# Chunked attention and a quadratic-relu FFN in one kernel: the first tiles' q and k are loaded four tokens to a partition and turned in 64x64 blocks

## The chip, the cores and the metric

The kernel runs on one core of one Trainium2 chip. The metric is the device time of one launch in microseconds, lower is better. The kernel before takes 829.1 us, the median of three runs (827.03 to 829.47). Engines are named as in the profile: PE is TensorE (matrix products), PEld its weight loads, DVE VectorE, ACT ScalarE, POOL GpSimd, SP the engine that issues most DMAs.

## The reference

Attention works inside chunks of 64 tokens, for 8 batches, 8 heads, 576 tokens and 64 channels. Its output, in token order, is the input of a feed-forward layer of 512 to 2048 to 512 with a quadratic ramp between.

```python
q_c, k_c, v_c = (x.reshape(B, H, nc, 64, D) for x in (q, k, v))
scores = q_c @ k_c.transpose(0, 1, 2, 4, 3) / sqrt(D)
attn = exp(scores - max(scores)); attn = attn / (sum(attn) + 1e-9)
x = (attn @ v_c).reshape(B, H, S, D).transpose(0, 2, 1, 3).reshape(B * S, H * D)
h = x @ w_in
g = where(h >= 1, h, where(h <= -1, 0, (h + 1) ** 2 / 4))
return g @ w_out
```

## The kernel before

**Tiles.** The 4608 tokens are cut into nine tiles of 512: tiles 0 to 5, 7 and 8 are the first 512 tokens of one batch each, tile 6 the last 64 tokens of all eight batches (`BATCH`). The attention of a tile is done in four head groups of two heads, each an array of 128 x 512. The feed-forward layer goes by 16 column blocks `j` of w_in and w_out. All its products are made from numbers split in a high and a low part, with three products in place of one.

**Attention of a group.** q and k arrive with tokens on the partitions and must have channels there. Three ways exist: PE multiplies by an identity matrix (`flip`, L436, four transposes of 128x128 for q and four for k) and ACT copies the result out (L461); or DVE transposes 32x32 blocks (L452) after a load in blocks (L371, L384 and others). `by_row(t, g)` says which: tile 0 and, of tile 1, the groups in `ROWED` go by PE. Then come the scores (L478), the exponent and its normalization (L552 to L570; by POOL at tile 0), the turning back of the weights (L436 with e, copied at L581), the product with v (L496), and the split of the result into xh (L613) and xl (L614).

**Feed-forward.** Tiles 0 to 2 run it directly: `ffn_in` (L665) and `ffn_out` (L700), twelve products of 128x512 for each block. Tiles 3 to 8 run in pairs with fewer products: `ffn_quad` (L880) works on combinations of weights that were mixed during tile 2 and written to DRAM (`mix_weights`, L761; read back L811), and half of its values are held in DRAM (L904) until the second tile of the pair recalls them (L939). The four token quarters of a tile accumulate in four PSUM banks, `ps_o` 0 to 3: 0 and 1 are tiles of their own, 2 and 3 one tile, `ps_o23`. At the end of a tile `store` evicts them, even quarters by ACT (L729), odd ones by DVE (L727), into the ring of four `tmp` buffers, which the held values use too, and SP sends them (L738).

**Weights** arrive in fp32 words by DMA (L296, L303) and are split by ACT and DVE in `prepare` (L320 to L342).

**The order.** A planner collects every piece of work with a cost and what it reads and writes, and lays the instructions out for each engine by estimated times, in the order they were added where it can; `plan.behind` ranks pieces later. While PE has no products in the start-up, it is filled with products of the identity (`warm`, L1105).

## Time and profile before

| | us |
|---|---|
| median of 3 runs | 829.1 |
| profiled execution | 828.9 |
| its span | 827.1 |
| PE busy | 819.0 (99%) |
| DVE busy | 563.2 (68%) |
| ACT busy | 422.5 (51%) |
| POOL busy | 153.8 (19%) |

The span is what the engines' records cover; the rest of the execution's time lies around it. Shares are means over stages: PE has work or filler nearly throughout, DVE and ACT are near full in the first 130 us, while the weights are prepared, and half idle at the end. A row of the timeline gives start, duration, engine, line, operation, written<-read, and in brackets how long the engine was idle before, and what ended that.

### The profile page before, as it was taken

What the parts mean: (1) busy time and instruction counts of PE and PEld (TensorE: products, weight loads), DVE (VectorE), ACT (ScalarE), POOL (GpSimd) and SP (SyncE); (2) the same over time, 40 slices, a digit from 0 to 9 for tenths busy, and PEclk for the clock granted to TensorE, in tenths of its full rate; (3) what the DMA queues carried; (4) which work ended last, traced back from release to release, by engine and by line L of the source; (5) the groups of instructions that cost most, each with busy time, mean ns of one, the idle gap of its engine ahead of it and who ended that gap; (6) DMA issues with size and microseconds to landing.
All of it is one profiled execution on the core that took longest, in us unless ns stands there. A gap on an engine that the chain in (4) does not pass through costs nothing.

```text
span 827.1 us, 15446 instructions
## 1 busy us (share of the span) xinstructions
PE 819.0 (99%) x5786; PEld 676.7 (82%) x5786; DVE 563.2 (68%) x965; ACT 422.5 (51%) x723; POOL 153.8 (19%) x278
## 2 busy tenths in 40 slices
PE   9999999999999999999999999999989999999998
PEld 8778878888888888888888888888878888888886
DVE  4889998857778888786787748775756254454422
ACT  5899965444445465455464344544544254454422
POOL 1222112222221111112122111121122121121220
PEclk9999999999999999999999999999999999999999
DMA  9998886554697546979597738875663264552432
GB/s 203 285 314 294 247 195 156 137 124 101 170 242 150 124 102 175 260 179 262 167 226 231 175 108 214 216 190 188 164 223 95 63 207 157 168 169 86 157 98 77
DMA packets 278683, 146.80 MB, mean 177 GB/s; under 512 B 243152, under 2 KB 251600, under 8 KB 278608
## 3 DMA queue, kind: packets, MB, share of 16 engines
q1 hardware_dynamic: 251584, 61.25, 33.7%
q0 software_dynamic: 24768, 83.90, 31.0%
q10 hardware_dynamic: 2256, 0.66, 0.5%
q8 instruction: 46, 0.75, 0.4%
q14 instruction: 29, 0.24, 0.1%
HBM read 101.71 MB, written 36.70 MB: 167 GB/s over the span
## 4 chain that ended last, share of the span: by engine, by line
PE 88%; DMA 4%; issue 2%; DVE 2%; SPq 2%; POOL 1%; ACT 0%; ACTq 0%; POOLq 0%; DVEq 0%
PE ps_o L700 43%; PE ps_h L880 26%; PE ps_h L665 13%; PE ps_a L478 2%; PE ps_h L496 2%; PE ps_a L700 1%; DMA words_wo<-in_moe_w_out_dram 1%; DMA v_sb<-in_v_dram 1%; DMA q_sb<-in_q_dram 1%; SPq L409 1%; DMA held<-tmp 1%; SPq L359 1%; DMA k_sb<-in_k_dram 1%; PE ps_a L436 0%; PE ps_o L665 0%
## 5 line engine op out<-in xcount | busy, mean ns | idle before, releaser
L700 PE MATMUL ps_o<-parts_wo,gh 128*128 128x512 f32 x1120 | 347.9, 392 | 2.2 <-DVE tmp L727 2.2
L700 PEld LDWEIGHTS ps_o<-parts_wo,gh 128*128 128x128 f32 x1120 | 208.6, 188 | 46.2 <-DVE tmp L727 2.8
L700 PE MATMUL ps_o<-parts_wo,gl 128*128 128x512 f32 x560 | 218.4, 390 | 0.0
L880 PE MATMUL ps_h<-big_wi,big_wi 128*128 128x512 f32 x720 | 172.3, 389 | 0.0
L880 PEld LDWEIGHTS ps_h<-big_wi,big_wi 128*128 128x128 f32 x720 | 135.2, 188 | 28.0
L665 PE MATMUL ps_h<-xh,parts_wi 128*128 128x512 f32 x376 | 125.4, 394 | 0.1
L686 DVE TENSOR_TENSOR gl<-r,gh 128x512 fp32r<-128x512 f32 x120 | 82.4, 687 | 60.9 <-ACT gh L685 60.1
L700 PEld LDWEIGHTS ps_o<-parts_wo,gl 128*128 128x128 f32 x560 | 105.2, 188 | 22.4 <-DVE gl L686 0.3
L685 ACT CAST gh<-r 128x512 fp32r<-128x512 f32 x120 | 74.2, 619 | 96.0 <-PE ps_o L700 55.8
L811 POOL DMA_DIRECT2D big_wi<-mixed x84 | 44.9, 535 | 264.1 <-PE ps_h L880 251.7
L665 PEld LDWEIGHTS ps_h<-xh,parts_wi 128*128 128x128 f32 x376 | 70.6, 188 | 16.1 <-DVE r L676 0.5
L665 PE MATMUL ps_h<-xl,parts_wi 128*128 128x512 f32 x188 | 73.6, 391 | 0.4 <-DVE xl L614 0.4
L894 ACT ACTIVATE tmp<-big_wi 128x512 f32<-128x512 f32 x48 | 30.3, 632 | 71.4 <-DVE big_wi L889 70.0
L880 PE MATMUL ps_h<-xh,big_wi 128*128 128x512 f32 x192 | 63.5, 390 | 0.0
L672 ACT ACTIVATE r<-ps_h 128x512 f32<-128x512 f32 x47 | 27.9, 597 | 43.6 <-PE ps_h L665 43.4
L889 DVE TENSOR_TENSOR big_wi<-ps_h,big_wi 128x512 f32<-128x512 f32 x48 | 32.9, 685 | 19.0 <-PE ps_h L880 13.8
L898 DVE SCALAR_TENSOR_TENSOR tmp<-big_wi,tmp 128x512 f32<-128x512 f32 x48 | 33.2, 692 | 15.9 <-ACT tmp L897 15.8
L676 DVE SCALAR_TENSOR_TENSOR r<-ps_h,r 128x512 f32<-128x512 f32 x47 | 32.1, 682 | 16.1 <-ACT r L675 15.9
L880 PEld LDWEIGHTS ps_h<-xh,big_wi 128*128 128x128 f32 x192 | 36.1, 188 | 7.7 <-DVE e L889 0.2
L665 PEld LDWEIGHTS ps_h<-xl,parts_wi 128*128 128x128 f32 x188 | 35.3, 188 | 7.7 <-DVE xl L614 0.7
L761 POOL DMA_DIRECT2D mixed<-e x32 | 17.2, 543 | 127.2 <-ACT e L790 127.2
L904 POOL DMA_DIRECT2D held<-tmp x48 | 26.4, 550 | 72.6 <-DVE tmp L898 72.5
(150 smaller groups left out, 1030.9 us busy)
## 6 DMA issues: line engine op xcount, KB each, us to landing
big_wi<-mixed POOLq DMA_DIRECT2D x84, 512.0 KB, 4.0
held<-tmp POOLq DMA_DIRECT2D x48, 256.0 KB, 3.8
words_wi<-in_moe_w_in_dram SPq DMA_DIRECT2D x16, 512.0 KB, 6.6
words_wo<-in_moe_w_out_dram SPq DMA_DIRECT2D x16, 512.0 KB, 7.5
out_dram<-tmp SPq DMA_DIRECT2D x31, 256.0 KB, 3.3
aT_both<-qT_both SPq DMA_DIRECT2D x112, 64.0 KB, 2.8
v_sb<-in_v_dram SPq DMA_DIRECT2D x52, 128.0 KB, 3.7
q_sb<-in_q_dram SPq DMA_DIRECT2D x104, 64.0 KB, 3.5
```

What stands on the lines that cost most here:

```text
L665: nc.tensor.matmul(out=ps, lhsT=weight["wi", j][:, half, kc * P:(kc + 1) * P], rhs=x, start=(kc == 0 and i == 0), stop=(kc == KC - 1 and i ...
L672: plan.add("act", 0.48, lambda: nc.scalar.activation(out=r, in_=ps, func=AF.Relu, bias=0.5, scale=0.5), (pkey,), (rkey,))
L676: plan.add("dve", 0.6, lambda: nc.vector.scalar_tensor_tensor(out=r, in0=ps, scalar=1.0, in1=r, op0=ALU.max, op1=ALU.min), (pkey,), (rkey,))
L685: plan.add("act", 0.52, lambda: nc.scalar.copy(out=gh, in_=r), (rkey,), (ghkey,))
L686: plan.add("dve", 0.6, lambda: nc.vector.tensor_tensor(out=gl, in0=r, in1=gh.bitcast(F32), op=ALU.subtract), (rkey, ghkey), (glkey,), port ...
L700: nc.tensor.matmul(out=acc, lhsT=x[:, cols], rhs=weight["wo", j][:, half, :], start=(j == 0 and i == 0), stop=(j == NF - 1 and i == 2),)
L811: plan.add("pool", 0.65, lambda: nc.gpsimd.dma_start(out=place_of(f"wi{slot}").bitcast(F32), in_=mixed[u]), keys, (f"wi{slot}_0", f"wi{slo ...
L880: nc.tensor.matmul(out=bank, lhsT=w[:, c:c + P], rhs=x()[:, kc, :], start=start and kc == 0 and k == 0, stop=kc == 1 and k == 2, skip_grou ...
L889: plan.add("dve", 0.6, lambda: nc.vector.tensor_tensor(out=out(), in0=bank, in1=x(), op=ALU.add), (key, xkey), (out_key,))
L894: plan.add("act", 0.5, lambda: nc.scalar.activation(out=r, in_=h(), func=AF.Relu, bias=0.5, scale=0.5), (hkey,), (rkey,))
L898: plan.add("dve", 0.6, lambda: nc.vector.scalar_tensor_tensor(out=r, in0=h(), scalar=1.0, in1=r, op0=ALU.max, op1=ALU.min), (hkey,), (rkey,))
L904: plan.add("pool", 0.65, lambda: nc.gpsimd.dma_start(out=held[j], in_=r), (rkey,), (f"held{j}",), lag=2.1, moving=0.8)
```

## The change

1. **Loads by rows.** `load_rows` sends one DMA for q or k of a group; partition p holds tokens 4p to 4p+3 of both heads, in runs of 1 KB. Before there were two DMAs (four at tile 1) with runs of 256 bytes. ACT issues k of groups 0 and 2, before of 0 and 1.
2. **Turning.** `flip_rows` turns q and k of a group together with 32 products of 64x64 blocks with the identity, into a pair of banks. The copies out of it put the tokens in order again: they write with a step of four elements. k of tile 0's groups 0 and 1 is copied by DVE, all other by ACT.
3. **Tile 1's group 1** goes by DVE's transposes instead of PE's.
4. **`ps_o` 0 and 1** become one tile of two banks, as 2 and 3 are.
5. **Start-up order.** The softmax is cut into `attn_exp` and `attn_norm`, and the stages of tile 0 stand in a string (T turn, S scores, A exponent, N normalization, B turn back, V product with v, X split, W split of weights). The turning back of groups 0 and 1 uses a bank of `ps_h`.
6. **`store`**: the last quarter of tiles 3, 5 and 7 is evicted to `e_bufs[0]` instead of the ring.
7. **`mix_weights`**: the three plain copies of a weight part to DRAM come behind the mixed ones and wait for their buffer.
8. One burst of attention stands at block 7 instead of 8, and softmax and turning back in a burst are ranked later by 22.

```diff
     FLIPPED, TURNED = 2, 1
-    ROWED = (0, 1)
...
-    o_pair, a_pair = bank_pair("ps_o23"), bank_pair("ps_a")
-    o_banks = buffers(psum, "ps_o", 2) + [(f"ps_o{2 + b}", o_pair[:, b, :]) for b in range(2)]
...
     def load_rows(dst, src, t, g, queue):
-        dst = dst.rearrange("p (c d) -> p c d", d=D)
-        for j in range(2):
-            queue.dma_start(
-                out=dst[j * C:(j + 1) * C],
-                in_=heads_rows(src, t, 2 * g + j).rearrange("c p d -> p c d"),
-            )
-    def load_halves(dst, src, t, g, queue):
-        dst = dst.rearrange("p (u r d) -> p u r d", r=2, d=D)
-        for j in range(2):
-            rows = heads_rows(src, t, 2 * g + j).rearrange("(r u) p d -> r p u d", r=2)
-            for r in range(2):
...
-            load = load_values if n == "v" else load_rows if t < TURNED else load_halves if by_row(t, g) else load_blocks
-            parts = (8 if t == TURNED else 4) if load == load_blocks else 4 if load == load_halves else 2
-            if BATCH[t] is None or (n, t) == ("v", TURNED):
+            load = load_values if n == "v" else load_rows if by_row(t, g) else load_blocks
+            parts = (8 if t == TURNED else 4) if load == load_blocks else 1 if load == load_rows else 2
+            if BATCH[t] is None or n == "v" and by_half(t, g):
...
-            issuer, queue = ("act", nc.scalar) if (n, t) == ("k", 0) and g < 2 else ("sp", nc.sync)
+            issuer, queue = ("act", nc.scalar) if (n, t) == ("k", 0) and g in (0, 2) else ("sp", nc.sync)
...
+    def flip_rows(pair, q_rows, k_rows):
+        for r in range(NS):
+            for n, x in enumerate((q_rows, k_rows)):
+                for a in range(2):
+                    for h in range(2):
+                        rows, at = slice(a * C, (a + 1) * C), h * HALF + r * D
+                        to = n * HALF + r * C
+                        nc.tensor.matmul(
+                            out=pair[h * D:(h + 1) * D, a, to:to + C],
+                            lhsT=x[rows, at:at + D], rhs=ident[rows, rows], start=True, stop=True,
+                        )
...
+    turned, ended = {}, {}
+    POOLED = (0, 1, 2, 3)
+    COPIED = ((0, 0, 1), (0, 1, 1))
...
+        pair, pkeys = ((o_pairs[0], ("ps_o0", "ps_o1")), (a_pair, ("ps_a0", "ps_a1")))[t]
+        plan.add("pe", 0.75, lambda: flip_rows(pair, *(src for (_, src), _ in sides)),
+                 [skey for (skey, _), _ in sides], pkeys, columns=1024, lag=0.0)
+        for n, (_, (dkey, dst)) in enumerate(sides):
+            by_dve = (t, g, n) in COPIED
+            eng = nc.vector.tensor_copy if by_dve else nc.scalar.copy
+            turned[n] = plan.add(
+                "dve" if by_dve else "act", 0.6 if by_dve else 0.48,
+                lambda n=n, dst=dst, eng=eng: eng(
+                    out=dst.rearrange("p (a u r) -> p a r u", a=2, r=NS),
+                    in_=pair[:, :, n * HALF:(n + 1) * HALF].rearrange("p a (r u) -> p a r u", r=NS),
+                ),
                 pkeys, (dkey,), lag=late(t, 1.5),
             )
             if t == 0:
-                turned[n] = copy
+                ended[0] = turned[n]
...
+    def attn_norm(t, g):
+        skey, sm = room("sm", sm_bufs, t, g)
+        ekey, e = e_room(t, g)
+        e3 = e.rearrange("p (n k) -> p n k", k=C)
...
-        on_pool = t < 1
+        on_pool = t == 0 and g in POOLED
...
-            pkey, ps = o_banks[1] if t == 0 else a_banks[0]
+            pkey, ps = (h_banks if g < 2 else o_banks)[1] if t == 0 else a_banks[0]
...
                 okey, o = (e_bufs[0], r_bufs[0])[by_dve]
+            elif t >= PAIRED and (t - PAIRED) % 2 == 0 and s == NS - 1:
+                okey, o = e_bufs[0]
             else:
...
-        for n, kc, which in ((i, 0, 1), (i, 1, 2), (j, 1, 4)):
-            to_mixed(m, which, [(None, keys[n], lambda n=n, kc=kc: weight["wi", n].bitcast(F32)[:, :, kc * HALF:(kc + 1) * HALF])])
...
+        for n, kc, which in ((i, 0, 1), (i, 1, 2), (j, 1, 4)):
+            to_mixed(m, which, [(None, (*keys[n], bkey), lambda n=n, kc=kc: weight["wi", n].bitcast(F32)[
+                :, :, kc * HALF:(kc + 1) * HALF
+            ])])
...
-        ("q", 0), ("k", 0), ("q", 1), ("k", 1), ("q", 2), ("k", 2), ("wi", 0), ("q", 3), ("k", 3),
-        ("v", 0), ("v", 1), ("wi", 1), ("v", 2), ("v", 3),
+        ("q", 0), ("k", 0), ("q", 1), ("k", 2), ("k", 1), ("q", 2), ("wi", 0), ("v", 1),
+        ("q", 3), ("k", 3), ("v", 0), ("wi", 1), ("v", 2), ("v", 3),
...
+    in_turn = (
+        "T0 S0 A0 T1 S1 N0 A1 N1 T2 S2 B0 V0 T3 S3 A3 A2 X0 B1 V1 N2 X1 B2 N3 B3 "
+        "V2 V3 W0 W2 X2 X3 W1"
+    )
+    for stage, n in in_turn.split():
+        stages[stage](int(n))
...
-    FIRST_SCORES, BURSTS = 4, (4, 8, 11, 15)
+    FIRST_SCORES, BURSTS = 4, (4, 7, 11, 15)
...
+        plan.behind = 22
         for at in then:
             attn_softmax(*at)
         if then:
             attn_turn_back_pair(then)
+        plan.behind = 0
```

SP's queue at the start, where the first loads are issued (L359 loads q and k, L296 weights, L409 v; `first_wi` are parts of weight space that hold groups 2 and 3). Before:

```order
L359 DMA q_sb_70<-in_q_dram 64x8x64 x2
L359 DMA q_sb_71<-in_q_dram 64x8x64 x2
L359 DMA first_wi_109<-in_q_dram 64x8x64 x2
L359 DMA first_wi_111<-in_k_dram 64x8x64 x2
L296 DMA words_wi_190<-in_moe_w_in_dram 128x4x256
L359 DMA first_wi_109<-in_q_dram 64x8x64 x2
L359 DMA first_wi_111<-in_k_dram 64x8x64 x2
L409 DMA v_sb_74<-in_v_dram 128x4x64 x2
L409 DMA v_sb_75<-in_v_dram 128x4x64 x2
```

And now (L360, L297, L401):

```order
L360 DMA q_sb_70<-in_q_dram 128x2x256
L360 DMA q_sb_71<-in_q_dram 128x2x256
L360 DMA k_sb_73<-in_k_dram 128x2x256
L360 DMA first_wi_108<-in_q_dram 128x2x256
L297 DMA words_wi_174<-in_moe_w_in_dram 128x4x256
L401 DMA v_sb_75<-in_v_dram 128x4x64 x2
L360 DMA first_wi_108<-in_q_dram 128x2x256
L360 DMA first_wi_110<-in_k_dram 128x2x256
L401 DMA v_sb_74<-in_v_dram 128x4x64 x2
```

Two DMAs of a tensor have become one; k of group 1 now goes by SP and k of group 2 by ACT, and v of group 1 comes ahead of group 3's q and k.

PE's first instructions after the warm-up, where group 0 of tile 0 is turned and its scores made (L436 and L478 before):

```order
L436 MATMUL ps_o_106<-ident,k_sb_72 128x128 x4
L1105 MATMUL ps_h_107<-ident 128x128
L436 MATMUL ps_o_105<-ident,q_sb_70 128x128 x4
L1105 MATMUL ps_h_107<-ident 128x128 x4
L478 MATMUL ps_a<-kT_78,qT_both 64x64 x16
L436 MATMUL ps_o_106<-ident,k_sb_73 128x128 x4
```

Now (L439 turns, L493 scores):

```order
L439 MATMUL ps_o_103<-ident,q_sb_70 64x64 x4
L439 MATMUL ps_o_103<-ident,k_sb_72 64x64 x4
...
L1130 MATMUL ps_h_106<-ident 128x128 x5
L493 MATMUL ps_a<-kT_78,qT_both 64x64 x16
L439 MATMUL ps_o_103<-ident,q_sb_71 64x64 x4
L439 MATMUL ps_o_103<-ident,k_sb_73 64x64 x4
```

The eight transposes of 128x128 into two tiles are now eight rows of four 64x64 products into one; the scores follow both.

DVE around the end of tile 5, with the engines and DMA queues whose work each instruction waits for (L727 is the eviction; `ps_o_106` and `ps_o_103` hold quarters 1 and 3 of the tile). Before:

```order
L898 SCALAR_TENSOR_TENSOR r_94<-e_80,r_94 128x512 [waits DVE_49,Activation_49]
L686 TENSOR_TENSOR gl_98<-r_94,gh_96 128x512 [waits PE_49,Activation_49]
L898 SCALAR_TENSOR_TENSOR tmp_99<-big_wi_161,tmp_99 128x512 [waits Activation_49]
L686 TENSOR_TENSOR gl_97<-r_93,gh_95 128x512 [waits DMASW5_49,PE_49,Activation_49]
L727 COPY tmp_101<-ps_o_106 128x512 [waits DMASW2_49,PE_49]
L686 TENSOR_TENSOR gl_98<-big_wi_161,gh_96 128x512 [waits DMASW1_49,PE_49,Activation_49]
L727 COPY tmp_99<-ps_o_103 128x512 [waits DMASW3_49,DVE_49,PE_49]
```

Now (L749; `ps_o_103` and `ps_o_104` are the two pairs):

```order
L921 SCALAR_TENSOR_TENSOR r_94<-e_80,r_94 128x512 [waits DVE_49,Activation_49]
L921 SCALAR_TENSOR_TENSOR tmp_99<-big_wi_160,tmp_99 128x512 [waits DVE_49,Activation_49]
L706 TENSOR_TENSOR gl_98<-r_94,gh_96 128x512 [waits PE_49,Activation_49]
L706 TENSOR_TENSOR gl_97<-r_93,gh_95 128x512 [waits DMASW7_49,PE_49,Activation_49]
L749 COPY tmp_101<-ps_o_103 128x512 [waits DMASW2_49,Activation_49]
L749 COPY e_80<-ps_o_104 128x512 [waits Activation_49]
L706 TENSOR_TENSOR gl_98<-big_wi_160,gh_96 128x512 [waits DMASW1_49,Activation_49]
```

Quarter 3 goes to `e_80` and no longer waits for a DMA; both evictions wait for ACT, where quarter 1 waited for PE; and they now stand next to each other, with one of the L686 rows (now L706) behind.

More of the change, by code (lines that the diff above doesn't have):

```diff
@@ L192 @@
     FLIPPED, TURNED = 2, 1
-    ROWED = (0, 1)
+    ROWED = (0,)
     EARLY = 2
@@ L238, in bank_pair @@
         return psum.tile([P, 2, T], F32, name=name)
-    o_pair, a_pair = bank_pair("ps_o23"), bank_pair("ps_a")
-    o_banks = buffers(psum, "ps_o", 2) + [(f"ps_o{2 + b}", o_pair[:, b, :]) for b in range(2)]
+    o_pairs, a_pair = [bank_pair("ps_o01"), bank_pair("ps_o23")], bank_pair("ps_a")
+    o_pair = o_pairs[1]
+    o_banks = [(f"ps_o{b}", o_pairs[b // 2][:, b % 2, :]) for b in range(4)]
     a_banks = [(f"ps_a{b}", a_pair[:, b, :]) for b in range(2)]
@@ L475, in product @@
             rows = slice(half * C, (half + 1) * C)
-            at = i * HALF + n * C if t == TURNED and not by_row(t, g) else (2 * n + i) * C
+            at = (i * HALF + n * C if by_half(t, g)
+                  else (n // 2 * 4 + 2 * i + n % 2) * C if by_row(t, g) else (2 * n + i) * C)
             at = slice(at, at + C)
@@ L492, in product @@
         def product(n, h, half):
-            at = (2 * n + h) * C if t < FLIPPED else h * HALF + n * C
+            at = (2 * n + h) * C if by_half(t, g) else h * HALF + n * C
             of = h * HALF + n * C
@@ L1111 @@
         (warm(h_banks[0][1]), None, plan.written["ps_h0"][0]),
-        (warm(o_banks[0][1]), turned[0], plan.written["ps_o0"][NP]),
+        (warm(o_banks[0][1]), ended[0], plan.written["ps_o0"][NP]),
     )))
```

62 lines of the change are left out of this document (26 added, 36 removed).

## The prediction

> **What bounds the kernel now.** I read the shares of busy time first, then TensorE's own list of waits, then stretches of the span.
>
> ```profile
> PE 819.0 (99%) x5786; PEld 676.7 (82%) x5786; DVE 563.2 (68%) x965; ACT 422.5 (51%) x723; POOL 153.8 (19%) x278
> ...
> PE ps_o L700 <- DVE tmp L727: 2.2, 1, 2.2
> PE ps_h L1105 <- POOL ident masks.py:199: 1.4, 1, 1.4
> PE ps_h L665 <- DVE xl L614: 0.4, 1, 0.4
> PE ps_a L436 <- DMA q_sb<-in_q_dram: 0.2, 1, 0.2
> ...
> 0.00:10.00 10.00, 8.64 (x83) 8.45 (x84) 0.83 (x2) 2.76 (x4) 0.70 (x6) 1.00 1.00 163
> 10.00:20.00 10.00, 9.88 (x192) 9.13 (x192) 8.10 (x18) 7.74 (x15) 2.48 (x3) 1.00 1.01 242
> 20.00:31.00 11.00, 10.64 (x144) 8.12 (x144) 9.56 (x18) 8.60 (x17) 4.08 (x5) 1.00 0.92 277
> 60.00:70.00 10.00, 10.00 (x76) 8.01 (x75) 8.64 (x16) 10.00 (x20) 1.45 (x2) 1.00 1.05 400
> 100.00:110.00 10.00, 10.00 (x104) 8.09 (x104) 10.00 (x19) 8.12 (x15) 1.45 (x2) 1.00 0.88 228
> 480.00:620.00 140.00, 137.82 (x1021) 113.84 (x1020) 94.51 (x155) 68.69 (x115) 26.93 (x50) 1.00 0.67 192
> 780.00:827.10 47.10, 43.28 (x190) 35.19 (x188) 12.10 (x18) 10.87 (x19) 5.91 (x11) 1.00 0.34 106
> ```
>
> TensorE is busy for 819.0 of 827.1 us. Its whole list of waits has four rows and 4.2 us, one of them a single wait of 2.2 us on an eviction by VectorE. The rows of stretches give span, then PE, PEld, DVE, ACT and POOL busy, granted clock, DMA share and GB/s. TensorE lacks 2.18 us between 480 and 620 and 3.82 at the end; the clock is 1.00 throughout. In the first 31 us a full PE means little, since it is filled with warm-up products on the identity (L1105). So time can change in three places only: the start-up until TensorE runs on real work, the few holes behind it, and the tail. Elsewhere only products removed or added count. The matmuls of 128x512 follow each other by 0.23 us (22.08 for 96 in the row below).
>
> **The change part by part.** *The hole at 616.*
>
> ```profile
> 606.75 0.68 DVE L898 SCALAR_TENSOR_TENSOR r<-e,r 128x512 f32<-128x512 f32 x1
> ...
> 612.27 0.55 POOL L904 DMA_DIRECT2D held<-tmp  x1
> ...
> 614.59 1.21 PE L496 MATMUL ps_h<-aT_both,v_sb 64*64 64x64 f32 x64
> ...
> 617.23 0.69 DVE L727 COPY tmp<-ps_o 128x512 f32<-128x512 f32 x1 [2.74 <-DMA held<-tmp]
> ...
> 617.98 0.73 PE L700 MATMUL ps_o<-parts_wo,gh 128*128 128x512 f32 x2 [2.18 <-DVE tmp L727]
> ...
> 612.27 4.84 DMA held<-tmp
> ...
> 617.98 22.08 PE ps_o L700 x96
> ```
>
> The eviction of tile 5's last quarter needs a buffer of the tmp ring, and that buffer's content is still being written to DRAM: issued at 612.27, landed 4.84 later, at 617.11. TensorE has finished the value products of L496 at 615.80 and stands until 617.98. For tiles 3, 5 and 7 the change sends just this quarter to e_bufs[0]. Its last use in this pair is the row at 606.75, and VectorE stands idle for 2.74 us before 617.23, that is from 614.49, so the wait is gone, unless VectorE has something else ahead of it. **−2.2 us.** Cases of tiles 3 and 7 show no DMA wait on TensorE's list, and gain nothing. What is late next is the ordinary order of the evictions, which the next item makes longer.
>
> *Accumulators 0 and 1 in one pair of banks.* Their evictions, one by ScalarE, one by VectorE, no longer overlap each other's products: VectorE's now waits for ScalarE's, and ScalarE's for the products of both. Accumulators 2 and 3 are such a pair already, so the trace has a price.
>
> ```profile
> 779.49 0.59 ACT L729 COPY tmp<-ps_o 128x512 f32<-128x512 f32 x1 [1.45 <-PE ps_o L700]
> 780.11 0.69 DVE L727 COPY tmp<-ps_o 128x512 f32<-128x512 f32 x1 [1.29 <-ACT tmp L729]
> 780.42 0.39 PE L700 MATMUL ps_o<-parts_wo,gl 128*128 128x512 f32 x1
> ...
> 780.86 0.73 PE L700 MATMUL ps_o<-parts_wo,gh 128*128 128x512 f32 x2
> ...
> 610.62 0.59 ACT L729 COPY tmp<-ps_o 128x512 f32<-128x512 f32 x1 [0.28 <-PE ps_o L700]
> ...
> 611.30 0.69 DVE L727 COPY tmp<-ps_o 128x512 f32<-128x512 f32 x1 [0.24 <-PE ps_o L700]
> ...
> 612.46 0.62 PE L700 MATMUL ps_o<-parts_wo,gh 128*128 128x512 f32 x2
> ```
>
> At 780.42 to 780.86 two products stand 0.44 apart instead of 0.23: 0.21 us for one such chain. For accumulators 0 and 1 at 611: the products of accumulator 1 end at about 611.26, ScalarE takes 0.59 and VectorE 0.69 with some 0.04 between each, which reaches 612.66, against 612.46 when the next product on that bank is due now. That is 0.2 us again. It comes up where the next tile's products follow at once, behind tiles 1, 3, 5 and 7: 4 x 0.22 = **+0.9 us**. Below: 0 where the scheduler put other work between. Above: all eight boundaries, 1.8.
>
> *The tail.*
>
> ```profile
> 821.33 0.59 ACT L729 COPY tmp<-ps_o 128x512 f32<-128x512 f32 x1 [3.00 <-PE ps_o L700]
> ...
> 821.94 1.69 SPq L738 DMA_DIRECT2D out_dram<-tmp  x3
> ...
> 823.82 0.33 SPq L738 DMA_DIRECT2D out_dram<-r  x1
> ```
>
> ScalarE's first eviction waits for accumulator 1 too, about 0.68 us (the next quarter's products end that much later), and SP's three sends of 0.56 each begin at 822.6 instead of 821.94. They then run to 824.3, and the last send by SP moves from 823.82 to 824.3: **+0.5 us**; 0 if the ScalarE queue's own last send, which does not move, ends later.
>
> *Tile 1, group 1 by VectorE.*
>
> ```profile
> 53.12 0.63 PE L436 MATMUL ps_a<-ident,q_sb 128*128 128x128 f32 x4 [0.18 <-DMA q_sb<-in_q_dram]
> 53.51 0.71 PE L700 MATMUL ps_o<-parts_wo,gh 128*128 128x512 f32 x2
> ...
> L452 DVE STREAM_TRANSPOSE qT_both<-q_sb x30: 668/699/712, 76.0 to 549.6; 128x512 f32<-128x512 f32 x30
> ```
>
> Two groups cost TensorE four turns now, each 0.39 by the start of what follows (53.51 − 53.12), so 1.56 us, plus the wait of 0.18. One group in the new form is 32 products of 64x64 for q and k together. The row at 614.59 has that many in 1.21 (the trace records each product on float32 operands of this size twice, x64). So −1.74 + 1.21 ≈ **−0.5 us**. VectorE gains two transposes of 0.70. It is full there (10.00 of 10 from 100 to 110), so the cover is thin: nothing if TensorE has other products queued, 1.4 if all of it passes through. I take +0.3, near the lower end, since no TensorE wait on VectorE appears now between 31 and 615.
>
> *Start-up.* Three edits meet here.
>
> ```profile
> 6.95 0.60 PE L436 MATMUL ps_o<-ident,q_sb 128*128 128x128 f32 x4
> ...
> 7.59 0.58 ACT L461 COPY qT_both<-ps_o 128x512 f32<-128x512 f32 x1
> ...
> 8.37 0.70 PE L478 MATMUL ps_a<-kT,qT_both 64*64 64x64 f32 x32
> ...
> 28.03 0.66 ACT L320 ACTIVATE tmp<-words_wo 128x512 f32<-128x512 f32 x1 [1.24 <-DMA words_wo<-in_moe_w_out_dram]
> ...
> 30.64 0.50 PE L665 MATMUL ps_h<-xl,parts_wi 128*128 128x512 f32 x1 [0.36 <-DVE xl L614]
> ...
> L326 ACT ACTIVATE words_wi<-words_wi 128x512 uint32<-128x512 uint32 x16 | 10.9, 679 | 0.0
> ...
> L338 ACT CAST parts_wi<-tmp 128x512 fp32r<-128x512 f32 x16 | 10.0, 624 | 1.7 <-DVE tmp L331 1.7
> ```
>
> (1) Loads. The DMA engines are full in the first 10 us (share 1.00) at 163 GB/s, and full at 400 GB/s between 60 and 70, with other pieces. The first q and k are in 256-byte pieces now and in 1024-byte ones after. They let the turn of q start at 6.95 today; between no gain and the whole ratio of the rates I take 4.8 to 5.3 for both tensors. (2) Turn and copies. Today they are two turns of 0.60, and ScalarE copies the one while TensorE turns the other. The new turn is one row of 1.2, and behind it k's copy (VectorE, 0.69) and q's (ScalarE, 0.59) follow each other, since they read one pair of banks. The first scores come at about 5.0 + 1.2 + 0.7 + 0.6 + 0.2 = 7.7 instead of 8.37. (3) The same lengthening comes three times more, for groups 1 to 3, while DVE is busy 9.56 and ACT 8.60 of 11 us from 20 on; so what the first group gains is paid back in part. Against it, the weights no longer queue behind slow pieces and the early DMA copies of POOL, and ScalarE's wait of 1.24 at 28.03 goes. What counts is when the product at 30.64 runs, since TensorE has no further wait until 53.12: I take **−0.2 us**, from −2.5 (loads and the wait passed through in full) to +4 (below).
>
> *A rule that speaks against it.* The copies that undo the order write with a step of 16 bytes. The nearest row is L326, which steps by 8 bytes on both sides: 0.679 against 0.624 of the contiguous L338, so a step of 8 costs 9%; I price the copies as today, plus 0.05. The Trainium skill ("Advanced Engine Details and Errata", "SBUF Cachelines") says that accesses should hit a 16-byte line at least twice, and that a new line with each access is penalized; at a step of 16 every element has its own line. By this rule the copies would take longer by an amount that the page doesn't state, which is the case of the second rival below; by the row the sum stays as it is. No copy with this step is in the trace of before, so the trace neither agrees nor disagrees.
>
> *POOL's late copies* to DRAM and the burst list: POOL is idle in most of the span (19% busy), and its reads of mixed weights wait for TensorE.
>
> ```profile
> L811 POOL DMA_DIRECT2D big_wi<-mixed x84 | 44.9, 535 | 264.1 <-PE ps_h L880 251.7
> ```
>
> 251.7 of the 264.1 us ahead of these reads are waits on TensorE, so a copy that comes later is covered; without that cover each costs its 0.54 of issue. I take 0.
>
> **Sum**: 828.9 (the profiled execution; span 827.1 and 1.8 around it) − 2.2 + 0.9 + 0.5 − 0.5 + 0.3 − 0.2 = 827.7. The profiled execution lies 0.2 under the median of the runs, 829.1.
>
> **The rivals.** *The loads carry through* (0.30). The start-up is bound by what the DMAs land, as share 1.00 in 0 to 10 and ScalarE's wait at 28.03 say. Then about 2.5 us come off in place of 0.2: 827.7 − 2.3 = 825.4. Against it: ACT and DVE are near full from 20 to 31, so an early landing meets a queue.
>
> *The strided copies are twice as long* (0.12): the side on which the kernel becomes slower. Eight copies of tile 0 at 1.2 instead of 0.59 to 0.69, six on ScalarE and two on VectorE, lie one behind the other in the chain of turn, scores and exponent, with ScalarE idle only 2.4 us between 20 and 31. 8 x 0.55 = 4.4, less 0.4 of idle that I let absorb it: 827.7 + 4.0 = 831.7. It decides from about 1.6 times the length on, where the loss passes the hole that was closed. For it: nothing in this trace writes by 16 bytes. Against: step 8 costs 9% only.
>
> *VectorE becomes the bound of tile 1* (0.11): two more transposes where it is full, 1.4 instead of 0.3, and the attention of tile 1 late by as much: 828.8.
>
> *The hole stays* (0.07): the eviction waits for something else, for example ScalarE's of its pair or the send that emptied e_bufs[0] last: 827.7 + 2.2 = 829.9. The row at 606.75 speaks against it.
>
> **How the numbers follow.** The forecast keeps 0.40, with 826.4 to 828.9 for its own range. 0.3% of 829.1, about what a measurement of this kernel can tell from no change, is 2.5 us: faster is below 826.6, slower above 831.6. Faster: 0.27 of the carried-through loads and a fifth of the forecast, 0.35. Slower: 0.09 of the strided copies and 0.03 of the others, 0.12. The same: 0.53. The range of 8 in 10 reaches from the loads' case with no price for the pair of banks (825.4 − 0.9 = 824.5) to just under the strided copies at full length, 831.3.
>
> **What would show it.** The hole: no row of TensorE waiting on an eviction near 615, and the eviction writes e. The pair: gaps of 0.2 behind ScalarE's evictions, four of them. The start: the copies by their mean duration (0.6 or 1.2), the first scores at 7.7, no wait of ScalarE on words_wo, and the last product that waits on xl at 30.4 instead of 30.64. Tile 1: a TensorE row waiting on a VectorE transpose or its scores near 95 would be the third rival. The forecast is wrong if the product that ends the start-up moves by more than 1 us either way, or if a new wait above 1 us stands anywhere on TensorE's list.

## The result

The changed kernel takes **836.4 us** (median of six runs, 834.23 to 838.1), the kernel before 828.6 in the same session (six runs, 827.03 to 832.57). The ratio is **1.0091**, 95% interval 1.0071 to 1.0111: slower by 7.8 us, where 827.7 and a range up to 831.3 were forecast. The profiled execution took 837.1, its span is 835.3.

The shares of busy time in the page of the changed kernel, and the five longest of TensorE's eight waits:

```profile
PE 823.3 (99%) x6066; PEld 680.1 (81%) x6066; DVE 564.4 (68%) x969; ACT 422.4 (51%) x719; POOL 153.7 (18%) x278
```

```profile
PE ps_o L493 <- issue: 2.0, 1, 2.0
PE ps_h L1130 <- POOL ident masks.py:199: 1.4, 1, 1.4
PE ps_a L493 <- ACT qT_both L472: 1.0, 1, 1.0
PE ps_h L903 <- DVE e L912: 0.9, 1, 0.9
PE ps_o L493 <- ACT first_wi L472: 0.8, 1, 0.8
```

TensorE has 280 instructions more (5786 before). The 2.2 us on the eviction at the end of tile 5 are gone. New are waits for the copies of the turned q and k (L472), one on VectorE's e, and one of 2.0 us with nothing named as its cause ("issue"). All but that on e lie in the first 25 us (the three that are not shown are of 0.3 to 0.4, in the start-up too). TensorE's timeline there (start, duration, engine, line, operation, written<-read):

```profile
1.37 5.07 PE L1130 MATMUL ps_h<-ident 128*128 128x128 f32 x22 [1.37 <-POOL ident masks.py:199]
6.36 0.41 PE L439 MATMUL ps_o<-ident,q_sb 64*64 64x64 f32 x8
...
9.89 0.69 PE L493 MATMUL ps_a<-kT,qT_both 64*64 64x64 f32 x32 [0.99 <-ACT qT_both L472]
...
21.97 0.68 PE L493 MATMUL ps_o<-first_wi,first_wo 64*64 64x64 f32 x26 [0.77 <-ACT first_wi L472]
24.69 0.49 PE L493 MATMUL ps_o<-first_wi,first_wo 64*64 64x64 f32 x6 [2.04 <-issue]
...
27.83 2.75 PE L1130 MATMUL ps_o<-ident 128*128 128x128 f32 x12
...
40.03 0.39 PE L685 MATMUL ps_h<-xl,parts_wi 128*128 128x512 f32 x1
```

The first scores begin at 9.89 (8.37 before), those of group 3 at 21.97 (18.18). These 32 rows are the 16 products of the program: the trace has two instructions for each of them, as for the products of the turns and the fillers, and the counts below are of such instructions. Behind the 26th TensorE stops for 2.04 us. The 12 filler instructions after it take 2.75; in a run below the same 12 take 1.50. The last row is the 20th product of 128x512, the one that stood at 30.64 before: 9.4 us late. The copies, in ScalarE's and VectorE's rows of this kernel:

```profile
7.66 1.09 DVE L472 COPY kT<-ps_o 128x512 f32<-128x512 f32 x1 [7.66 <-PE ps_o L439]
...
8.78 1.05 ACT L472 COPY qT_both<-ps_o 128x512 f32<-128x512 f32 x1 [5.71 <-DVE kT L472]
```

They take 1.05 to 1.13. Before, ScalarE's took 0.57 to 0.59; VectorE had none, and its copies of 128x512 out of PSUM take 0.69. The stretches (span; PE, PEld, DVE, ACT, POOL busy; clock, DMA share, GB/s):

```profile
15.00:20.00 5.00, 4.24 (x168) 3.86 (x162) 3.67 (x8) 3.54 (x6) 0.93 (x1) 1.00 0.90 287
20.00:25.00 5.00, 2.19 (x60) 1.78 (x52) 2.15 (x4) 4.09 (x6) 1.04 (x1) 0.86 1.02 352
25.00:30.00 5.00, 5.00 (x25) 4.61 (x21) 3.84 (x9) 1.67 (x3) 1.57 (x2) 0.50 1.09 373
30.00:35.00 5.00, 5.00 (x66) 4.09 (x68) 2.65 (x6) 3.40 (x6) 0.51 (x1) 0.96 1.07 397
```

From 20 to 25 TensorE is busy for 2.19 of 5 us, and from 25 to 30 the granted clock is 0.50. That is why fillers and products take nearly twice as long there. The DMA engines are full from 20 on.

How late the big products (128x512) of the changed kernel are against the same products before, counted in the two traces:

| product | before, us | after, us | late by |
|---|---|---|---|
| 1st | 21.91 | 26.40 | 4.5 |
| 20th | 30.64 | 40.03 | 9.4 |
| 50th | 37.60 | 46.83 | 9.2 |
| 200th | 75.67 | 86.75 | 11.1 |
| 500th | 154.37 | 161.47 | 7.1 |
| 1600th | 421.79 | 428.93 | 7.1 |
| 2000th | 516.96 | 524.59 | 7.6 |
| 2400th | 612.23 | 621.38 | 9.2 |
| 2500th | 638.53 | 645.79 | 7.3 |
| end of span | 827.12 | 835.32 | 8.2 |

Behind the 50th the change gains 1.0 us in all: 2.1 until the 500th, 1.9 at the hole of tile 5, less 0.5, 1.5 and 0.9. The whole loss is made in the first 31 us of the kernel before. A single trace is good to about 1 us there: in three runs below that have the start-up of the kernel before (the eviction buffer, items 6 and 8, and the same order), the 20th product stands at 29.4 to 29.8 and not at 30.64.

### The profile page after: what moved, and what is told of

Same layout as the page of the kernel before. It is cut to its first block, busy times and chain, and to the rows that moved or that the text cites. A ratio compares the mean times of both kernels' runs of the same rounds, so it can differ in the third digit from the quotient of the medians.

```text
span 835.3 us, 15975 instructions
## 1 busy us (share of the span) xinstructions
PE 823.3 (99%) x6066; PEld 680.1 (81%) x6066; DVE 564.4 (68%) x969; ACT 422.4 (51%) x719; POOL 153.7 (18%) x278
## 4 chain that ended last, share of the span: by engine, by line
PE 96%; ACT 1%; DMA 1%; DVE 1%; SPq 1%; issue 1%; POOL 0%; POOLq 0%; DVEq 0%
PE ps_o L720 46%; PE ps_h L903 26%; PE ps_h L685 16%; PE ps_a L493 2%; PE ps_h L511 2%; PE ps_a L720 1%; DMA aT_both<-qT_both 1%; PE ps_h L1130 1%; PE ps_o L1130 1%; SPq L614 1%; PE ps_o L439 1%; ACT first_wo L472 0%; PE ps_o L685 0%; PE ps_a L511 0%; PE ps_o L493 0%
## 5 line engine op out<-in xcount | busy, mean ns | idle before, releaser
L706 DVE TENSOR_TENSOR gl<-r,gh 128x512 fp32r<-128x512 f32 x120 | 82.2, 685 | 68.7 <-ACT gh L705 68.0
```

The lines of the kernel that those rows point to most:

```text
L706: plan.add("dve", 0.6, lambda: nc.vector.tensor_tensor(out=gl, in0=r, in1=gh.bitcast(F32), op=ALU.subtract), (rkey, ghkey), (glkey,), port ...
```

## The experiments

Ratios are against the kernel before, run on the same chip (medians 828.4 to 829.6), with their 95% intervals.

### Copies and loads

The theory after the first look: the copies' stores with a step of 16 bytes are the loss.

**Copies without a step.** Source and destination contiguous.

```diff
-                    out=dst.rearrange("p (a u r) -> p a r u", a=2, r=NS),
-                    in_=pair[:, :, n * HALF:(n + 1) * HALF].rearrange("p a (r u) -> p a r u", r=NS),
+                    out=dst.rearrange("p (a x) -> p a x", a=2),
+                    in_=pair[:, :, n * HALF:(n + 1) * HALF],
```

> The changed kernel with its order of instructions kept; only the copies behind the new turns write straight on instead of with a step of 16 bytes. They leave out putting the tokens of tile 0 and of tile 1's first head group back in order, so those rows of the output are other rows. Copy theory (the copies of 1.09 us instead of 0.59 set the start-up, and the hole and half clock of TensorE around 23 to 30 us are their consequence): copies at 0.6, third scores some 3 us earlier, the twentieth big product near 32 instead of 40, clock 1.00, 828 to 829 us. Fetch theory (TensorE runs out of fetched instructions at 22.65, whatever the copies take, and the clock halves for it): copies at 0.6, but a gap of about 2 us inside a group of score products stays and the mean clock stays under 0.998: 832 us. If the copies stay at 1.09, the step isn't their cause: 836.

**The step on the side of the read.** The order is undone while reading PSUM; the store is contiguous.

```diff
-                    out=dst.rearrange("p (a u r) -> p a r u", a=2, r=NS),
-                    in_=pair[:, :, n * HALF:(n + 1) * HALF].rearrange("p a (r u) -> p a r u", r=NS),
+                    out=dst.rearrange("p (a u r) -> p a u r", a=2, r=NS),
+                    in_=pair[:, :, n * HALF:(n + 1) * HALF].rearrange("p a (r u) -> p a u r", r=NS),
```

> The changed kernel with its order kept; the copies put the tokens in order by reading PSUM with a step of 64 elements and writing straight on. Result as the reference's. If only the write's step of 16 bytes costs: copies 0.6 and the time of the run with plain copies. If any step costs, in PSUM too: copies near 1.1 and 836 us.

**Fewer products.** 16 products of 128 rows and 64 columns instead of 32 of 64x64, with copies as in the change.

```diff
-        for r in range(NS):
-            for n, x in enumerate((q_rows, k_rows)):
-                for a in range(2):
...
-                            lhsT=x[rows, at:at + D], rhs=ident[rows, rows], start=True, stop=True,
+        for n, x in enumerate((q_rows, k_rows)):
+            for r in range(NS):
...
+                        out=pair[h * D:(h + 1) * D, n, r * P:(r + 1) * P], lhsT=x[:, at:at + D], rhs=ident, start=True, stop=True,
```

> The changed kernel with 16 products of 128x64 with 128 columns per group for the turn instead of 32 of 64x64 with 64 columns; copies as in the change (step of 16 bytes), other work the same. Copy theory: the turn is a little shorter, 835 to 836, hole and half clock stay. Fetch theory: 80 instructions fewer before 22 us, the hole of 2.0 us inside the score products is gone or comes later, clock nearer 1.00, 831 to 832.

Measured: 836.2 (1.0077, 1.0052 to 1.0103), 835.0 (1.0065, 1.0047 to 1.0082) and 837.3 (1.009, 1.0067 to 1.0114). The copies of the second kernel by group (count, shortest/median/longest in ns), and then its timeline at the place of the hole:

```profile
L472 ACT COPY first_wo<-ps_o x3: 586/586/587, 9.8 to 17.0; 128x512 f32<-128x512 f32 x3
L472 DVE COPY kT<-ps_o x1: 691/691/691, 7.4 to 7.4; 128x512 f32<-128x512 f32 x1
```

```profile
18.22 0.68 PE L493 MATMUL ps_o<-first_wi,first_wo 64*64 64x64 f32 x26
21.77 0.49 PE L493 MATMUL ps_o<-first_wi,first_wo 64*64 64x64 f32 x6 [2.88 <-issue]
```

Reading with the step costs nothing (0.59 and 0.69); the step of the stores cost 0.5 and 0.4 each. Group 3's scores begin at 18.22, as before the change. But the hole behind the 26th instruction is now 2.88 us. In the first run it is at the same instruction, 3.70 long and ends at 23.66. So most of the gain of the copies goes into the hole. Against the kernel before of its own session the second run is slower by 5.5 us, the changed kernel by 7.8: 2.3 are gained, with intervals of 1.5 and 1.7 to either side. 828 to 829 were expected, and the theory of the copies alone falls. (The profiled execution of the second run is the fastest of its eight, so its trace shows the hole rather too short.)

The third run has no hole in that place, but its turn takes longer:

```profile
16.70 1.97 PE L437 MATMUL ps_o<-ident,first_wi 128*64 128x128 f32 x32
```

1.97 instead of 1.11 for q and k of a group. The 64x64 products in four quarters of the array overlap (in the changed kernel the first four start at 6.36, 6.37, 6.37 and 6.38), these do not. So this edit does not stand for "fewer instructions" alone.

**Both undone.** Fewer products and the step on the read.

> The changed kernel with both suspects taken away at once: 16 turns of 128x64 per group instead of 32 of 64x64, and copies that write straight on (they read PSUM with a step). Two-cause theory (slow copies and the late block of instructions hide each other, since the chain that is behind arrives at the block's boundary later): no hole marked issue above 0.5 us on TensorE, clock 1.00, copies 0.6, the twentieth big product at 31 to 33 us instead of 35.9 with the copies alone and 38.9 with the turns alone; time 829 to 831 us, 5 to 7 less than the changed kernel. Rival (the order of the stages itself is slower): the start-up stays 5 us or more behind, 834 or more.

Measured: 836.9 (1.0102, 1.0084 to 1.012), where 829 to 831 were expected. There is no hole, and the 20th product stands at 35.77, with turns of 1.97 each: not at 31 to 33, but 4.3 earlier than in the changed kernel. The time shows nothing of it, since this kernel loses 4.3 us between the 2000th and the 2400th product, where the changed one loses 1.5. A wait of 1.81 on VectorE's e ends there at 526.7, and the granted clock is half for 3.4 us behind it.

**What the hole is.** In the changed kernel and the first two runs the hole falls behind the same instruction, whenever TensorE gets there (18.9 to 22.7 us). What arrives shortly ahead of its end is a record of 16 KB in the queue of instruction blocks. Two stretches of the changed kernel's DMA queues, 16 to 22 us (first row) and 22 to 23.5 us (the others): packets, MB, share of the engines.

```profile
q1 hardware_dynamic: 1225, 1.96, 92.4%
...
q1 hardware_dynamic: 435, 0.44, 92.0%
q8 instruction: 1, 0.02, 3.7%
```

The record starts at 22.20, and TensorE goes on at 24.69. In the first run the two are at 21.46 and 23.66, in the second at 19.53 and 21.77. Ahead of it the engines carry data alone. A count says the same. In the fifteen traces of this document TensorE has 19 waits above 0.1 us that are marked "issue". Of these, 16 stand behind 193 of its recorded instructions (weight loads counted) or behind a multiple of 256 more, this one behind the 961st; the other three, all later than 580 us, stand one instruction further. 256 instructions in a record of 16 KB are 64 bytes each. The theory: TensorE has used up its instructions, and the next block waits for its turn in full DMA engines. The rival: something else stops TensorE at this product, and the loads have nothing to do with it.

**Loads held.** As the second run, and SP waits, ahead of the loads of the third w_in block and all later ones, for a 4-byte DMA that reads group 3's turned q. So no weights are under way when the block is due.

```diff
+    def gate(key, x):
+        scratch = dram.tile([1, 1], F32, name="gate")
+        plan.add("sp", 0.5, lambda: nc.sync.dma_start(out=scratch, in_=x[0:1, 0:1]), (key,), ("gate",))
+        held_until.append("gate")
...
+        if stage + n == "T3":
+            gate(*first["qT", 3])
```

> The kernel with copies that read with a step, the same instructions on TensorE up to the hole, and one edit: SP waits, by a DMA of four bytes that reads the fourth group's turned q, before it issues the weights wo0, wi3, wo1 and what follows. So fewer bytes are under way from 14 to 18 us. Queue theory (the 16 KB block of TensorE's instructions stands in the DMA engines behind up to eight transfers): the block's record comes earlier than 19.5 us, the hole of 2.9 us shrinks to under 1 us, clock near 1.00, 831 to 833 us against 835. Count theory (too many small instructions, whatever the DMA engines do): record and hole stay, 835 or more, since the weights come later.

**Loads held, copies slow.** The same gate on the changed kernel itself.

> The changed kernel itself (copies with the step of 16 bytes, 32 turns per group) with SP held back as in the run e6, order of TensorE the same as there. It takes the late block of instructions away alone. If hole and half clock are the larger cause: no hole above 1 us near 22, clock 0.999 or more, 831.5 to 833.5 us against the 836.4 of the change. What is left over the 830.6 of e6 is what the slow copies cost once the hole no longer hides them: 1 to 4 us. If the time stays at 836, the loads under way aren't the cause in the changed kernel.

Measured: 830.6 (1.0032, 1.0019 to 1.0045) and 832.0 (1.004, 1.0024 to 1.0056). TensorE's rows at the hole and the stretches of the first of these:

```profile
19.03 0.68 PE L500 MATMUL ps_o<-first_wi,first_wo 64*64 64x64 f32 x26
20.66 0.34 PE L500 MATMUL ps_o<-first_wi,first_wo 64*64 64x64 f32 x6 [0.96 <-issue]
...
22.40 1.50 PE L1140 MATMUL ps_o<-ident 128*128 128x128 f32 x12
```

```profile
15.00:20.00 5.00, 4.51 (x167) 3.93 (x167) 2.81 (x7) 3.80 (x8) 1.04 (x1) 1.00 0.52 132
20.00:25.00 5.00, 4.34 (x64) 3.94 (x63) 4.77 (x11) 3.49 (x7) 1.04 (x1) 1.00 0.90 340
```

and of the second at the same product:

```profile
20.49 0.69 PE L500 MATMUL ps_o<-first_wi,first_wo 64*64 64x64 f32 x32 [0.79 <-ACT first_wi L479]
```

The block comes at 18.00, when the loads have drained, and the hole shrinks to 0.96; in the second, where TensorE reaches the place later, it is gone, and the 32 products stand in one row. The clock stays at 1.00. The four kernels make a square; in brackets, how much slower each is than the kernel before of its own session:

| | loads as changed | loads held |
|---|---|---|
| stores with the step | 836.4 (7.8) | 832.0 (3.5) |
| stores contiguous | 835.0 (5.5) | 830.6 (2.1) |

By the brackets the loads are worth 4.4 and 3.4, the stores 2.3 and 1.4, each give or take about 2 us by the intervals. The loads are clear of that, the stores are hardly: with the loads held, the traces have the 20th product at 33.99 and 33.81, only 0.2 apart. The rival falls: without these loads under way the hole shrinks or goes. Holding them shows no cost of its own: with them held no engine waits for a DMA from 10 to 50 us.

That it is the instruction block that they hold back is read from the records and the count; no run moved the block alone. The record of the block that begins behind the 961st instruction starts 3.5 to 4.6 us after the 705th instruction in the three kernels with the hole, and 1.4 and 0.7 after it with the loads held.

The loads are only half of the cause. In the kernel before the DMA engines are as full (1.01 and 0.92 in the prediction's rows from 10 to 31 us), and the same record starts 5.5 us after the 705th instruction, at 28.94. But there TensorE needs the block only at 44.4, and here at 22.65: on its small products 256 instructions last 3.9 us, where before they last 21. The two runs with 16 products for a turn, whose loads are as in the change, need it at 35.2 and 32.1, its record starts at 28.68 and 25.90, and they have no hole.

### What is left of the start-up

With both causes gone the 20th product stands at 33.81, still 3.2 late. The delay arises behind the first big product, which is not late (21.61, before 21.91). The products with v of groups 1, 2 and 3 begin at 23.82, 28.02 and 29.43, before at 21.29, 23.02 and 27.01, and fillers run in between. Three theories were tried, each on the kernel with loads held and contiguous stores (e6, or the sixth run, in the texts of the expectations).

**Fewer fillers ahead of the first turn.** The changed kernel's q has landed by 5: its loads are issued at 0.7 and 1.3 and take

```profile
L360 SPq DMA_DIRECT2D q_sb<-in_q_dram x2: 441/445/449, 0.7 to 1.3; - x2
...
DMA to landing us min/median/max: 3.9/4.3/4.7
```

but its 22 filler instructions run from 1.37 until 6.4. They follow each other by 0.21 us, later ones by 0.11, and the planner counts them all alike. Here it counts them double for the first 3.4 us.

```diff
-                    free[fill_engine] = self.products_end(free[fill_engine], fill_cost, fill_columns)
+                    cold = 2 if free[fill_engine] < self.START + 3.4 else 1
+                    free[fill_engine] = self.products_end(free[fill_engine], fill_cost * cold, fill_columns)
```

> The kernel of e6 (copies that read with a step, loads held) with the planner told that a filler product takes twice as long in the first 3.4 us, as the trace shows; so 7 fillers stand ahead of the first turn instead of 11, and some others move. q and k are in SBUF at 4.6 to 5.0 us while the first turn starts at 5.6 to 6.4. If the fillers hold up the start-up: first turn at 5.0, the twentieth big product 1 us earlier or more, 829.5 us. If the chain of copies and scores decides: 830.6 as e6.

Measured: 833.3 (1.0045, 1.0029 to 1.0061). The first scores begin at 7.67, which is the time of the forecast, but the second group's at 11.46, and the 20th product at 33.06. An early first group buys 0.75 us there. By the 50th product it is gone (41.18 against 40.96), and waits of 1.8 us on evictions behind it take more.

**The stages in their old order.**

```diff
-        "T0 S0 A0 T1 S1 N0 A1 N1 T2 S2 B0 V0 T3 S3 A3 A2 X0 B1 V1 N2 X1 B2 N3 B3 "
-        "V2 V3 W0 W2 X2 X3 W1"
+        "T0 S0 A0 N0 T1 S1 A1 N1 T2 S2 A2 N2 B0 V0 X0 T3 S3 A3 N3 B1 V1 X1 B2 V2 "
+        "X2 B3 V3 X3 W0 W1 W2"
```

> The kernel of e6 (copies that read with a step, loads held) with the stages of tile 0 in the order of the kernel before (turn, scores, exponent, normalization of a group; turning back, values and split two groups behind). In e6 the maximum of group 2 (VectorE, from the bank pair of its scores) runs only behind the value product of group 0, which goes into the same pair: 18.3 us, though its scores were made by 16.4. If this order is what is left of the slow start: that maximum near 16.5, the normalized weights of groups 2 and 3 some 2 us earlier, the twentieth big product at 31 to 32 us instead of 33.8, 828 to 829 us. If the turns and their serial copies are it: 33.5 or later, and 830 to 831.

Measured: 831.7 (1.0044, 1.0031 to 1.0056), 20th product at 33.41. Group 2's maximum runs at 16.93, near the 16.5 that the theory asked for, and the start-up is as late as it was. This wait, and the order by itself, are not the cause.

**q and k turned into banks of their own.**

```diff
-        plan.add("pe", 0.75, lambda: flip_rows(pair, *(src for (_, src), _ in sides)),
-                 [skey for (skey, _), _ in sides], pkeys, columns=1024, lag=0.0)
+            k_pkeys, k_pair = bank_pair_of(t, g)
+        for n, keys in enumerate((pkeys, k_pkeys)) if t == 0 else ():
+            plan.add("pe", 0.375, lambda n=n: flip_rows(pair, k_pair, (n,), *(src for (_, src), _ in sides)),
+                     (sides[n][0][0],), keys, columns=512, lag=0.0)
```

> The changed kernel with the copies reading with the step (as in the second run) and the loads held (as in the sixth), and one more edit: for tile 0 the turn of q stays in the banks ps_o0 and ps_o1, but the turn of k goes into the pair of banks in which the same group's scores will stand, as a piece of its own, so that each copy waits for its own turn alone and the two copies share no bank. Theory (the 3 us that are left at the 20th big product, 33.81 in the sixth run against 30.64 before, are the serial turn and copies of each group: 2.6, 3.0, 2.8 and 2.4 us from the turn's start to the scores, against 2.08, 1.9, 1.9 and about 2.0 before): each group then takes 2.0 to 2.2, the sum of the excess falls from 2.9 to under 0.8, the 20th product comes at 31 to 32.2 and the time falls from 830.57 to 828.4 to 829.3. Rival (the groups are set by VectorE's and ScalarE's softmax steps and by the landing of the loads, and the turn's own length is hidden): the 20th product stays at 33.3 or later, and the time at 830 to 831.5.

Measured: 835.5 (1.0073, 1.0044 to 1.0102), 20th product at 36.42.

```profile
5.50 1.09 PE L448 MATMUL ps_a<-ident,k_sb 64*64 64x64 f32 x32
...
8.07 0.69 PE L510 MATMUL ps_a<-kT,qT_both 64*64 64x64 f32 x32
...
10.49 0.69 PE L448 MATMUL ps_o<-ident,first_wi 64*64 64x64 f32 x30
13.00 0.27 PE L448 MATMUL ps_o<-ident,first_wi 64*64 64x64 f32 x2 [1.81 <-issue]
...
14.86 1.13 PE L510 MATMUL ps_o<-first_wo 64*64 64x64 f32 x32
```

The first group, the only one that nothing disturbs, takes 2.57 from turn to scores as it did with one pair (2.60), which speaks against the theory. For the rest the run decides nothing. The planner now puts group 2's turn ahead of group 1's scores, an earlier block is late in it (a hole of 1.81), and group 1's scores come at 14.86. **The last 3 us of the start-up stay open.**

### The late parts alone

**The eviction buffer.** The kernel before with item 6.

```diff
+            elif t >= PAIRED and (t - PAIRED) % 2 == 0 and s == NS - 1:
+                okey, o = e_bufs[0]
```

> The kernel before with one edit of the change: the last quarter of tiles 3, 5 and 7 goes to the e buffer. My forecast's step: the hole of 2.18 us at 616 is gone, nothing else moves, 2.2 us less than before (826.9 by the profiled run). Rival: the eviction waits for something else and the time stays.

Measured: 829.3 (0.9993, 0.9981 to 1.0005). The hole of tile 5 closes (1.9 us between the 2400th and the 2500th product), but 2.6 are lost between the 1600th and the 1800th, where before and change have no wait. VectorE's rows of this kernel there:

```profile
449.19 0.68 DVE L563 TENSOR_REDUCE sm<-kT 128x8 f32<-128x512 f32 x1
...
450.23 0.63 DVE L563 TENSOR_REDUCE sm<-kT 128x8 f32<-128x512 f32 x1
...
452.39 1.30 DVE L601 STREAM_TRANSPOSE qT_both<-kT 128x512 f32<-128x512 f32 x2
453.61 0.65 DVE L686 TENSOR_TENSOR gl<-big_wi,gh 128x512 fp32r<-128x512 f32 x1
454.18 0.68 DVE L686 TENSOR_TENSOR gl<-r,gh 128x512 fp32r<-128x512 f32 x1
```

The planner, which is given other buffers, now lays the softmax of two groups in a row, and gl, which the output products need, comes at 453.61. TensorE waits for it twice, 0.67 and 0.50 us. In the kernel before it stands at 450.32:

```profile
450.32 0.68 DVE L686 TENSOR_TENSOR gl<-big_wi,gh 128x512 fp32r<-128x512 f32 x1
```

What looks like one edit is two.

**Items 6 and 8.** Also block 7 for a burst and the rank of 22.

```diff
-    FIRST_SCORES, BURSTS = 4, (4, 8, 11, 15)
+    FIRST_SCORES, BURSTS = 4, (4, 7, 11, 15)
...
+        plan.behind = 22
```

> The kernel before with the eviction to the e buffer and the change's burst edits (block 7 instead of 8, softmax ranked later by 22). In the run with the eviction alone the hole at 616 went, but VectorE made both groups' softmax in a row around 447 to 453 and TensorE then waited for L686. If the ranking is what keeps that from coming: no wait on L686 there, hole gone, 826.5 to 827.5 us. If not: 829 as with the eviction alone.

**Items 3, 4, 6, 7 and 8.** All of the change but its start-up.

```diff
-    ROWED = (0, 1)
+    ROWED = (0,)
...
-    o_pair, a_pair = bank_pair("ps_o23"), bank_pair("ps_a")
+    o_pairs, a_pair = [bank_pair("ps_o01"), bank_pair("ps_o23")], bank_pair("ps_a")
...
+            elif t >= PAIRED and (t - PAIRED) % 2 == 0 and s == NS - 1:
+                okey, o = e_bufs[0]
```

> The kernel before with the parts of the change that lie behind the start-up: eviction buffer, burst edits, pair of banks, late copies to DRAM, tile 1's second group by VectorE; loads, turns, copies and stage order of tile 0 as before. My forecast's terms for these: -2.2 +0.9 +0.5 -0.5 +0.3, so 827.9. If they hold, the whole loss of the change is its start-up. If it comes out above 829.5, the pair or the transposes cost more than I said.

Measured: 832.9 (1.0053, 1.0033 to 1.0073) and 832.1 (1.0053, 1.0033 to 1.0073); neither of the expected times came. In the first of them the wait on gl near 454 us and the hole at 616 are gone, as the ranking was to bring, but new waits stand at 116 to 121 us (2.0 on parts_wo, 0.7 on gl) and at 234 (0.7). Its costliest wait, and the four costliest late ones of the second:

```profile
PE ps_o L700 <- DVE parts_wo L342: 2.0, 2, 1.4
```

```profile
PE ps_h L497 <- DVE r L677: 1.3, 1, 1.3
PE ps_o L701 <- DVE tmp L730: 0.9, 1, 0.9
PE ps_h L885 <- DVE e L894: 0.8, 1, 0.8
PE ps_h L885 <- DVE r L903: 0.8, 1, 0.8
```

From the 50th product to the end of the span the late part loses 4.4 us with the old start-up (0.8 late, then 5.2, in an execution 1.9 above its median); with the new one it gained 1.0 (9.2, then 8.2). The new waits are on VectorE, at other places than in the changed kernel. So these runs give the late edits no price of their own: what they cost depends on the order that the planner then lays.

**The eviction buffer in the same order.** To price the hole alone, only tile 5's last quarter is sent to e, after the ring has counted on as before: the other buffers and every instruction's place stay as they were. (In the trace the order of TensorE, VectorE and ScalarE is that of the kernel before; the one instruction that differs is this eviction.)

```diff
+                if t == 5 and s == NS - 1:
+                    o = e_bufs[0][1]
```

> The kernel before with one buffer changed and not one instruction moved: the last quarter of tile 5 goes to the e buffer, while the planner and the tmp ring still count it as before. My forecast's first term by itself: no wait on the eviction at 616, TensorE 1.9 to 2.2 us earlier from there on, 826.6 us (ratio 0.9975). If the order of instructions was not what took the gain back in e4 and e7, the time stays at 828.5 to 829.

Measured: **826.6** (0.9976, 0.996 to 0.9993), faster than both kernels.

```profile
615.77 1.21 PE L496 MATMUL ps_h<-aT_both,v_sb 64*64 64x64 f32 x64
615.88 0.69 DVE L729 COPY e<-ps_o 128x512 f32<-128x512 f32 x1 [0.21 <-PE ps_o L700]
...
616.91 0.72 PE L700 MATMUL ps_o<-parts_wo,gh 128*128 128x512 f32 x2
```

The products follow the value products at once; between the 2400th and the 2500th big product 2.25 us are gone, as the forecast's first term said (2.2). The time falls by 2.0.

## Why the prediction was wrong

**The hole at 616 (−2.2)** was right: 1.9 in the changed kernel, 2.25 by itself.

**The rest behind the start-up** was right in sum and not by its terms. *Tile 1, group 1* was to give 0.2 net; by the 500th product the change has gained 2.1 (9.2 to 7.1 late). Which of the moved instructions gives it was not tried. *The pair of banks* was to cost 0.9 at four boundaries; one of them shows 0.5 (between the 1600th and the 2000th product), the others nothing. *The tail* was to cost 0.5: SP's last send stands 0.47 further behind the last product than before, and the span ends 0.9 further. What the sum did not have is a wait of 0.9 on VectorE's e, in a stretch that loses 1.5. Together −1.0, against −1.0 forecast (−2.2 + 0.9 + 0.5 − 0.5 + 0.3). That the sums agree is luck: the terms do not, and a trace is good to about 1 us.

**Start-up, step (2): the copies.** "I price the copies as today, plus 0.05" was wrong: 1.05 to 1.13 instead of 0.59 to 0.69. The row of L326, with a step of 8 bytes, was no bound for a step of 16. The second rival had the length right. Its price was too high: 4.0 was forecast, and the stores cost 2.3 in the time, or 1.4 with the loads held, each by about 2 us to either side. They put group 3's scores off by 1.46 us where the loads were held (20.49 against 19.03), and by 3.75 in the changed kernel (21.97 against 18.22), where the hole behind took up most of it. With the loads held, 0.2 of it reaches the 20th product. The Trainium skill ("Advanced Engine Details and Errata", "SBUF Cachelines") had the direction: a new 16-byte line with each access is penalized. For stores the trace agrees, with a factor of 1.6 to 1.9; what the step costs in reading PSUM was 0.

**Start-up, step (1): the loads.** The earlier landing was right: q's turn could have begun at 5.0. It did not, since the fillers run to 6.36, which could have been seen in the order: they stand ahead of the turn as a fixed number. And it would have bought little: with fewer fillers the first scores came at 7.67, and the time did not fall.

**Start-up, steps (2) and (3): what is late next.** This is the step that failed by most. The start-up was put at −0.2, and by the 20th product it was 9.4 late; 1 us was the prediction's own sign of being wrong. Step (2) priced the new turn by TensorE's time alone, "one row of 1.2", and put its instructions at nothing. Step (3) said that the weights no longer queue behind slow pieces, and counted this as a gain. ScalarE's wait for words_wo at 28.03 did go, as it said; the rival *the loads carry through* had the same sign.

The loads in large pieces do run at 310 to 358 GB/s from 5 to 15 us (212 and 236 before). But the engines are full from 15 to 25 us all the same (0.90 and 1.02), as they were before, and the many small products (6066 instructions in place of 5786) bring TensorE to the end of its block at 22.65 instead of 44.4. It stands still for 2.0 us (2.9 and 3.7 in the runs with quick copies), and the clock is half for 3.4 to 6.8 us. Taking the loads away from that moment brings 4.4 us in the changed kernel; with fewer instructions the hole is gone without that. The text had quoted "share 1.00" as a sign that loads bound the start, and did not ask what else goes by the same engines, nor how soon TensorE would need it.

The sum by what was measured: 828.6 − 1.0 (late terms) + 1.4 (stores, with the loads held) + 4.4 (loads and the block, with the clock) gives 833.4. The 3.0 that are missing to 836.4 are the open remainder of the start-up, which the 20th product of the run with loads held and contiguous stores shows as 3.2. In the traces' 20th product the same parts are 0.2, 6.0 and 3.2 of the 9.4.

## What to carry to other kernels

Count a faster load as a load on the DMA engines at a given moment, and look up what else must pass there then; in a start-up that is also the instruction stream of the busiest engine. Count that engine's instructions too: a product split into small ones may take no longer and yet use up the block sooner. If an order must be undone in a copy out of PSUM, put the step on the read and keep the store contiguous. And where a planner orders the work, price a small edit with the order held fixed, since a change of one buffer moved other work by more than the edit was worth.

## What the runs showed of the hardware

- **Instruction blocks are late beside data.** Records of 16 KB in the queue of instructions belong to 256 instructions of TensorE. Beside full DMA engines the one for the 961st started 3.5 to 5.5 us after the 705th instruction in the change, the first two runs and the kernel before, with the loads held 0.7 and 1.4. TensorE went on 2.2 to 2.7 us after such a record began. Where the 256 ahead of the 961st lasted 3.1 to 3.9 us beside full engines, it stood still for 2.0 to 3.7 us, with the loads held for 0.96 and 0; where they lasted 21, not at all. The Trainium skill ("Runtime: NRT & Kernel Launch", "Instruction fetch mechanics") calls the cost of crossing such a block mostly hidden; here it was not, in the part that was shown above.
- **The clock fell after some short holes.** Holes of 1.81 (twice), 2.04, 2.88 and 3.70 us were followed by half clock for 3.4, 3.4, 6.8, 3.4 and 6.8 us. But the hole of 2.18 at 616 in the kernel before was not, nor one of 0.96. So the length of the hole alone does not decide it, and no run here tells what else does.
- **A store with a step of 16 bytes** takes 1.05 to 1.13 us for 128x512, a contiguous one with the same step on the side of PSUM 0.59 (ScalarE) and 0.69 (VectorE).
- **Small products overlap.** Turning q and k of a group by 32 products of 64x64 in four quarters of the array takes 1.11 us, by 16 products of 128 rows 1.97.
